# Attention and a feed-forward layer on one core: all weights converted during attention, x prepared in small pieces, each token tile visited once

## The chip, the core and the metric

The kernel runs on one core of one Trainium2 chip. The metric is the device time of one execution in microseconds, the median of 3 runs. The engines named below are those of the profile: PE (TensorE matmul, with its weight loads as PEld), DVE (VectorE), ACT (ScalarE), POOL (GpSimd) and SP (SyncE, whose queue issues every DMA here). Each engine runs its own instructions in order and waits for semaphores of the others.

## The reference

Causal attention with a decay over 8 batches x 8 heads x 576 positions x 64, then a feed-forward layer with a gate of its own on the 4608 tokens x 512:

```python
scores = (q @ k.T) / sqrt(64) + cum[:, None] - cum[None, :]     # cum = cumsum(log(clip(f, 1e-4, 1)))
attn = softmax(where(causal, -1e9, scores));  x = attn @ v       # -> 4608 tokens x 512
h = x @ w_in                                                     # 512 x 2048
out = (h * erf(softplus(h))) @ w_out                             # 2048 x 512
```

The weights arrive as 64-bit floats, and the kernel turns them into 32-bit floats itself with integer operations on the two words of each. Every feed-forward operand is split into a high part that TensorE multiplies as fp32r and a low part, and a product is three matmuls (high x high, high x low, low x high). The first product uses Strassen's scheme in Winograd's form: 7 products of halves instead of 8, so weights and x are combined (sums and differences of halves) before they are split.

## The kernel before, in words

**Attention** is a software pipeline over t = 0..68. One head pair has two values of t, 64 in all. In iteration t the kernel scales the probabilities of t-2 (normalize: two small DVE operations, L493 and L494, then 4 or 6 POOL operations, L498), copies out the result of t-5 (store), computes the scores of t (PE), reduces them on DVE while it adds the decay (L476), exponentiates those of t-1 (ACT), transposes those of t-3 (PE, copied out by ACT and DVE) and multiplies those of t-4 by v (PE). The result goes to xt_d in DRAM. At the end of an iteration stands one step of weight conversion: convert(u, step) for quarter u = 4a + i of the eight feature blocks a, four steps to a quarter. Half the weights (16 quarters, blocks 0 to 3) are converted here, from t = 4 on; they go to DRAM as wi_d[a] and wo_d[a].

**The feed-forward stage** is a list of 48 units, each one token tile (768 tokens) with one feature block (256 of 2048). In middle(u) PE does down(u), 36 matmuls of 512 columns into y; ACT does softplus and erf for unit u+1 (activate), DVE adds y into ys (flush, L250) and multiplies the gate (L210), ACT and POOL split the gate into gh and gl (round_gate, L217 and L218). Then PE does up(u+2), 42 matmuls of 384 columns. So PE alternates down and up, and gl(u+1) has to be there when down(u+1) begins.

The units are ordered in nine visits: tiles 0 to 2 with blocks 0 to 3, tiles 0 to 2 again with blocks 4 to 7, then tiles 3 to 5 with all eight. The partial sums of the first three visits go to DRAM (part_d) and are read back (want_y). In the first eleven units tasks() puts six conversion steps into each unit, for the other 16 quarters. x of the next visit is loaded with xt_d two units ahead (load_x), combined on POOL (combine_x, 768-element operations, L125) and split by split_x (ACT copies the high part, L144, POOL or DVE subtract it, L145), all of this around the last unit of a visit. For the first visit it is done in iterations 58 to 63 of attention.

The order on PE, DVE, ACT and POOL is the order in which the code is written; SP's order is left to a scheduler. Tile pools set who has to wait for a buffer: wop (the feed-forward layer's wo tiles), yp and ps_y are opened only when attention's pools are closed, on the same memory.

## Time and profile before

| | |
|---|---|
| median of 3 runs | 1215.16 us (1213.96 to 1215.73) |
| the profiled execution: time, span | 1214.0 us, 1212.2 us |
| mean granted TensorE clock | 0.965 |
| PE, DVE, ACT, POOL busy, share of the span | 91%, 68%, 58%, 54% |
| HBM read, written | 231.88 MB, 46.81 MB |
| down(0) begins; the last two downs run together (from the span's start) | 396.05 us; 16.38 us from 1192.12 |

How to read it: a row of a timeline has the start, the duration, the engine, the line, what is written and read, a count, and in brackets the engine's idle time ahead of it and who ended it. A row of a windows view has, for one stretch, its length, the busy time of PE, PEld, DVE, ACT and POOL with counts, the granted clock, the DMA engines' busy share and GB/s. The chain of waits follows the work that ended last back from the end: a row there is a start, a duration and what it was. A row of a group of instructions has its count, its summed time, the mean in ns of one, and the idle time ahead.

### The profile page before, as it was taken

What the parts mean: (1) busy time and instruction counts of PE and PEld (TensorE: products, weight loads), DVE (VectorE), ACT (ScalarE), POOL (GpSimd) and SP (SyncE); (2) the same over time, 40 slices, a digit from 0 to 9 for tenths busy, and PEclk for the clock granted to TensorE, in tenths of its full rate; (3) what the DMA queues carried; (4) which work ended last, traced back from release to release, by engine and by line L of the source; (5) the groups of instructions that cost most, each with busy time, mean ns of one, the idle gap of its engine ahead of it and who ended that gap; (6) DMA issues with size and microseconds to landing.
All of it is one profiled execution on the core that took longest, in us unless ns stands there. A gap on an engine that the chain in (4) does not pass through costs nothing.

```text
span 1212.2 us, 21632 instructions
## 1 busy us (share of the span) xinstructions
PE 1108.3 (91%) x7552; PEld 966.7 (80%) x7552; DVE 822.8 (68%) x1883; ACT 708.3 (58%) x1532; POOL 659.3 (54%) x691
## 2 busy tenths in 40 slices
PE   5999999999885968878779999999999999999998
PEld 3887878878674757767669888898999899989997
DVE  4788888888863667786856565656565666665565
ACT  3787777777774344545355655656556555665553
POOL 2566586585883575675673637283336533452233
PEclk7999999999998889888979999999999999999999
DMA  6689889798565458768669594948545855556532
GB/s 243 195 263 343 297 272 333 235 310 253 192 190 178 181 195 287 282 216 309 228 209 329 181 328 166 339 157 289 187 186 191 278 202 181 181 187 239 191 131 87
DMA packets 73420, 280.10 MB, mean 231 GB/s; under 512 B 7648, under 2 KB 16864, under 8 KB 61024
## 3 DMA queue, kind: packets, MB, share of 16 engines
q1 hardware_dynamic: 73312, 278.72, 66.3%
q8 instruction: 60, 0.98, 0.3%
q14 instruction: 48, 0.39, 0.1%
HBM read 231.88 MB, written 46.81 MB: 230 GB/s over the span
## 4 chain that ended last, share of the span: by engine, by line
PE 57%; POOL 18%; DVE 11%; issue 9%; DMA 3%; ACT 2%; SPq 0%; POOLq 0%; ACTq 0%; DVEq 0%
PE y L230 20%; PE s L453 7%; PE o L537 6%; PE pha L171 5%; PE phx L171 5%; PE phy L171 5%; PE t L510 5%; POOL gl L218 4%; POOL xs L145 4%; POOL rt L125 3%; DVE ys L250 2%; POOL pr L498 2%; PE phb L171 2%; POOL wa L381 2%; DVE e L210 2%
## 5 line engine op out<-in xcount | busy, mean ns | idle before, releaser
L218 POOL TENSOR_TENSOR gl<-e,gh 128x384 fp32r<-128x384 f32 x192 | 217.2, 1162 | 344.8 <-PE y L230 218.0
L230 PE MATMUL y<-wo,gh 128*128 128x512 f32 x1152 | 361.3, 395 | 30.1 <-DVE ys L250 17.2
L230 PEld LDWEIGHTS y<-wo,gh 128*128 128x128 f32 x1152 | 218.1, 191 | 76.4 <-DVE ys L250 20.2
L230 PE MATMUL y<-wo,gl 128*128 128x512 f32 x576 | 227.4, 395 | 0.0
L250 DVE TENSOR_TENSOR ys<-y,ys 128x512 f32<-128x512 f32 x252 | 172.9, 689 | 78.9 <-PE y L230 76.8
L498 POOL TENSOR_SCALAR pr<-pr,st 128x576 f32<-128x576 f32 (+4 forms) x320 | 166.6, 543 | 108.6 <-DVE st L494 96.9
L488 ACT ACTIVATE pr<-pr,st 128x576 f32<-128x576 f32 (+3 forms) x320 | 176.8, 557 | 8.4 <-DVE st L476 8.4
L476 DVE CUSTOM_DVE_ANT_0 pr<-s,c 128x576 f32<-128x576 f32 (+3 forms) x320 | 136.7, 487 | 51.9 <-PE s L458 44.8
L171 PE MATMUL pha<-xs,wi 128*128 128x384 f32 x576 | 123.6, 351 | 36.4 <-DVE u L181 35.5
L171 PEld LDWEIGHTS pha<-xs,wi 128*128 128x128 f32 x576 | 105.4, 195 | 45.6 <-DVE u L181 30.9
L217 ACT CAST gh<-e 128x384 fp32r<-128x384 f32 x192 | 92.3, 512 | 69.6 <-DVE e L210 69.2
L453 PE MATMUL s<-k,q 64*128 64x320 f32 (+4 forms) x768 | 117.3, 424 | 13.6 <-DMA k<-in_k_dram 8.3
L230 PEld LDWEIGHTS y<-wo,gl 128*128 128x128 f32 x576 | 109.6, 190 | 24.0 <-POOL gl L218 0.7
L171 PE MATMUL phx<-xs,wi 128*128 128x384 f32 x576 | 121.1, 346 | 0.3
L171 PE MATMUL phy<-xs,wi 128*128 128x384 f32 x576 | 118.7, 341 | 0.0
L510 PE MATMUL t<-ident,pr 128*128 128x128 f32 x800 | 106.8, 278 | 10.1 <-POOL pr L498 8.3
L519 ACT COPY pt<-t 128x512 f32<-128x512 f32 x128 | 73.6, 576 | 70.8 <-PE t L510 70.8
L200 ACT ACTIVATE e<-pha 128x384 f32<-128x384 f32 x48 | 23.5, 490 | 155.2 <-PE pha L171 155.2
L537 PE MATMUL o<-pt,v 128*64 128x128 f32 (+1 forms) x1920 | 104.6, 262 | 9.8 <-DVE xo L546 7.9
L177 DVE TENSOR_TENSOR u<-phx,u 128x384 f32<-128x384 f32 x96 | 53.6, 558 | 87.3 <-PE phx L171 85.1
L453 PEld LDWEIGHTS s<-k,q 64*128 64x128 f32 x768 | 77.0, 195 | 44.3 <-issue 28.3
L537 PEld LDWEIGHTS o<-pt,v 128*64 128x64 f32 x1920 | 95.8, 139 | 19.8 <-issue 6.5
(65 smaller groups left out, 1692.0 us busy)
## 6 DMA issues: line engine op xcount, KB each, us to landing
wi<-wi_d SPq DMA_DIRECT2D x48, 1792.0 KB, 7.4
wo<-wo_d SPq DMA_DIRECT2D x48, 1024.0 KB, 5.0
v<-in_vp_dram SPq DMA_DIRECT2D x32, 576.0 KB, 6.8
c<-cum_d SPq DMA_DIRECT2D x62, 288.0 KB, 5.5
r<-xt_d SPq DMA_DIRECT2D x36, 384.0 KB, 3.6
q<-in_q_dram SPq DMA_DIRECT2D x32, 320.0 KB, 4.4
k<-in_k_dram SPq DMA_DIRECT2D x32, 288.0 KB, 5.0
xt_d<-xo SPq DMA_DIRECT2D x32, 288.0 KB, 6.5
```

The lines of the kernel that those rows point to most:

```text
L171: nc.tensor.matmul(out=ps, lhsT=wi[:, w, n, kd], rhs=xs[:, x, kd], start=not part and kd == 0 and i == 0, stop=kd == 1 and i == 2, skip_gr ...
L217: nc.scalar.copy(out=gh, in_=e_)
L218: nc.gpsimd.tensor_tensor(out=gl, in0=e_, in1=gh.bitcast(F32), op=ALU.subtract)
L230: nc.tensor.matmul(out=y, lhsT=x[:, cs], rhs=wo[:, i, w], start=i == 0 and n == 0, stop=i == 1 and n == 2)
L250: nc.vector.tensor_tensor(out=ys, in0=y, in1=ys, op=ALU.add)
L453: nc.tensor.matmul(out=s[j][:, at:at + k1 - k0], lhsT=q[h, PAD + START[i]:PAD + END[i]], rhs=k[h, k0:k1], start=i > 0, stop=k1 < END[i])
L476: nc.vector.tensor_tensor_reduce(out=to[:, ::-1] if j else to, in0=score, in1=decay_, scale=-0.125, scalar=BIG, op0=ALU.add, op1=ALU.min, ...
L488: nc.scalar.activation(out=seg, in_=seg, func=AF.Exp, bias=st[:, 0, j, m:m + 1], scale=-1.0, accum_out=st[:, 1, j, m:m + 1])
L498: nc.gpsimd.tensor_scalar(out=seg, in0=seg, scalar1=st[:, 2, j, m:m + 1], scalar2=1.0, op0=ALU.mult, op1=ALU.mult)
L510: nc.tensor.transpose(out=b[:, n * P:(n + 1) * P], in_=probs[t][:, at:at + P], identity=ident)
L519: nc.scalar.copy(out=pt[:, 512 * a:512 * a + 512], in_=b)
L537: nc.tensor.matmul(out=o[h, to:to + width], lhsT=v[:, ch, h], rhs=pt[:, at[j]:at[j] + width], start=n == 0, stop=n == len(parts) - 1, skip ...
```

## The change

**Weights.** All 32 quarters are converted during attention, by a table of work with 70 slots: one slot at the end of each iteration from t = 4, two from t = 60 on. A quarter takes two slots: words (three DVE tensor_scalar operations) and joined (two DVE scalar_tensor_tensor operations), where before it took four steps with one POOL and four DVE operations. The combining and splitting of weights is cut into pieces over the following slots: combine (two 256-element POOL operations at a time), in_high and in_low (ACT, POOL: 512-element pieces in place of one of 1792 elements), out_high and out_low. The pool cv is closed with attention.

**x.** x_steps cuts the combining and splitting of one tile's x into 29 steps: 22 POOL operations of 384 elements and 7 ACT copies. For tile 0 they run one an iteration from t = 33; for the next tiles, prepare(u) puts up to five of them behind round_gate in the units a = 1 to 6 of the visit before. The pool xq gives odd tiles four more buffers. DVE takes no part in it any more.

**Visits.** There are six visits of eight units, so a tile's sums stay in ys, and part_d is gone.

```diff
...
-NU1 = 4
-HALF = 3
+X0 = 32
...
-TINY = float(np.array(0x38100000, np.uint32).view(np.float32))
+TINY = 2.0 ** -15
...
-        if part == 0:
...
+        def sub(name, a, b, kd):
+            if kd == 0 and name not in ("12",):
+                raw[v, name] = self.half(name, v)
+            nc.gpsimd.tensor_tensor(out=raw[v, name][:, kd], in0=raw[v, a][:, kd], in1=raw[v, b][:, kd], op=ALU.subtract)
+
+        def high(n, nm):
+            pool = self.xq if v % 2 and n > 2 else self.xp
+            self.xs[v, n] = x = pool.tile([P, 2, 2, TB], F32R, name=f"xs{v}_{n}", tag="xs",
+                                          bufs=10 if pool is self.xp else 4)
+            nc.scalar.copy(out=x[:, 0], in_=raw[v, nm])
+
+        def low(n, nm, kd):
+            x = self.xs[v, n]
+            nc.gpsimd.tensor_tensor(out=x[:, 1, kd], in0=raw[v, nm][:, kd], in1=x[:, 0, kd].bitcast(F32),
+                                    op=ALU.subtract)
+
+        steps = []
+        for name, a, b in (("T1", "12", "11"), ("T2", "22", "T1"), ("12", "22", "12")):
+            steps += [lambda args=(name, a, b, kd): sub(*args) for kd in range(2)]
+        for n, nm in enumerate(("11", "T2", "12", "T1", "21", "T4", "22")):
+            if n == 5:
+                steps += [lambda args=("T4", "21", "T2", kd): sub(*args) for kd in range(2)]
+            steps.append(lambda n=n, nm=nm: high(n, nm))
+            steps += [lambda args=(n, nm, kd): low(*args) for kd in range(2)]
+        return steps
...
-    def want_y(self, u):
...
-
     def flush(self, u, tb, y):
         nc = self.nc
-        k, a = self.units[u]
-        v, feats = self.visits[k]
-        ys = self.y[k][tb]
-        if a:
-            nc.vector.tensor_tensor(out=ys, in0=y, in1=ys, op=ALU.add)
+        v, a = divmod(u, NU)
+        if a == 0:
+            self.y[v, tb] = self.yp.tile([P, DM], F32, name=f"ys{v}_{tb}", tag="ys", bufs=8)
+            nc.vector.tensor_copy(out=self.y[v, tb], in_=y)
+            return
+        ys = self.y[v, tb]
+        nc.vector.tensor_tensor(out=ys, in0=y, in1=ys, op=ALU.add)
+        if a == NU - 1:
+            row = v * NW + tb * P
+            nc.sync.dma_start(out=self.out[row:row + P], in_=ys)
+
+    def prepare(self, u):
+
+        v, a = divmod(u, NU)
+        if v + 1 == NV:
+            return
+        if a == 0:
+            self.load_x(v + 1)
+            self.later = self.x_steps(v + 1)
         else:
-            nc.vector.tensor_copy(out=ys, in_=y)
-        if a == feats[-1]:
-            row = v * NW + tb * P
-            nc.sync.dma_start(out=self.out[row:row + P] if a == NU - 1 else self.part_d[v * NTB + tb], in_=ys)
-
-    def prepare(self, u):
...
-
-    def prepare_last(self, u):
...
-
-    def middle(self, u, tasks):
+            for _ in range(-(-len(self.later) // (NU - 1 - a)) if a < NU - 1 else 0):
+                self.later.pop(0)()
+
+    def middle(self, u):
...
         if more:
             for n in range(4):
                 self.round_gate(u + 1, n)
+            self.prepare(u)
...
-    cv = ctx.enter_context(tc.tile_pool(name="cv", bufs=2))
...
-    def convert(u, step):
...
+        cv = ph.enter_context(tc.tile_pool(name="cv", bufs=2))
...
+        def load_weight(u):
+
+            a, i = divmod(u, 4)
+            if a == NU:
+                return
+            r = (2 * a + i) * P
+            raw = cv.tile([P, 2 * DM], I32, name=f"wraw{u}", tag="wraw")
+            raws[u] = [raw.rearrange("p (n w) -> p n w", w=2)[:, :, w] for w in range(2)]
+            nc.sync.dma_start(out=raw, in_=w_in[a, i - 2] if i > 1 else w_out[r:r + P])
+
+        def words(u):
+
+            raw = raws[u]
+            tops[u] = top = cv.tile([P, DM], F32, name=f"wtop{u}", tag="wtop", bufs=3)
+            topi = top.bitcast(I32)
+            nc.vector.tensor_scalar(out=topi, in0=raw[1], scalar1=0x7FFFFFFF, scalar2=None, op0=ALU.bitwise_and)
+            nc.vector.tensor_scalar(out=top, in0=top, scalar1=TINY, scalar2=None, op0=ALU.max)
+            nc.vector.tensor_scalar(out=topi, in0=topi, scalar1=3, scalar2=0x3FFFFFFF,
+                                    op0=ALU.logical_shift_left, op1=ALU.bitwise_and)
+
+        def joined(u):
+
+            a, i = divmod(u, 4)
+            raw, topi = raws.pop(u), tops[u].bitcast(I32)
+            nc.vector.scalar_tensor_tensor(out=topi, in0=raw[0], scalar=29, in1=topi,
+                                           op0=ALU.logical_shift_right, op1=ALU.bitwise_or)
+            out_, top, sign = topi, topi, raw[1]
+            if i > 1:
+                if i == 2:
+                    sums[a] = cv.tile([P, 8, 2 * P], F32, name=f"wa{a}", tag="wa", bufs=1)
+                out_ = (sums[a][:, 4:6] if i == 3 else sums[a][:, ::7]).bitcast(I32)
+                top, sign = (x.rearrange("p (i n) -> p i n", i=2) for x in (top, sign))
+                del tops[u]
+            nc.vector.scalar_tensor_tensor(out=out_, in0=sign, scalar=-0x40000000, in1=top,
+                                           op0=ALU.bitwise_and, op1=ALU.bitwise_or)
+            load_weight(u + 2)
+
+        def out_high(a, i):
+            highs[a, i] = hi = cv.tile([P, DM], F32R, name=f"wohi{a}_{i}", tag="wohi", bufs=1)
+            nc.scalar.copy(out=hi, in_=tops[4 * a + i])
+            nc.sync.dma_start(out=wo_d[a][:, 2 * i * DM:(2 * i + 1) * DM], in_=hi.bitcast(F32))
+
+        def out_low(a, i):
+            top, hi = tops.pop(4 * a + i), highs.pop((a, i))
+            nc.gpsimd.tensor_tensor(out=top, in0=top, in1=hi.bitcast(F32), op=ALU.subtract)
+            nc.sync.dma_start(out=wo_d[a][:, (2 * i + 1) * DM:(2 * i + 2) * DM], in_=top)
+
+        def combine(a, *which):
+            w = sums[a]
+            for n in which:
+                x, y, op = {3: (7, 5, ALU.add), 2: (0, 7, ALU.subtract), 1: (3, 0, ALU.subtract),
+                            6: (4, 1, ALU.subtract)}[n]
+                nc.gpsimd.tensor_tensor(out=w[:, n], in0=w[:, x], in1=w[:, y], op=op)
+
+        def in_high(a, lo, hi):
+            highs[a] = part = cv.tile([P, 4, 2 * P], F32R, name=f"whi{a}_{lo}", tag="whi", bufs=1)[:, :hi - lo]
+            nc.scalar.copy(out=part, in_=sums[a][:, lo:hi])
+            nc.sync.dma_start(out=wi_d[a][:, lo * 256:hi * 256], in_=part.rearrange("p i f -> p (i f)").bitcast(F32))
+
+        def in_low(a, *which):
+            for lo, hi in which:
+                w = sums[a][:, lo:hi]
+                nc.gpsimd.tensor_tensor(out=w, in0=w, in1=highs[a][:, lo % 4:lo % 4 + hi - lo].bitcast(F32), op=ALU.subtract)
+                if hi == 7:
+                    nc.sync.dma_start(out=wi_d[a][:, 7 * 256:], in_=sums.pop(a)[:, :7].rearrange("p i f -> p (i f)"))
+
+        work = defaultdict(list)
+        for a in range(NU):
+            for i in range(4):
+                work[8 * a + 2 * i].append((words, 4 * a + i))
+                work[8 * a + 2 * i + 1].append((joined, 4 * a + i))
+            for i in range(2):
+                work[8 * a + 2 * i + 2].append((out_high, a, i))
+                work[8 * a + 2 * i + 3].append((out_low, a, i))
+            for n, args in enumerate([(combine, a, 3, 2), (combine, a, 1, 6), (in_high, a, 0, 4), (in_low, a, (0, 2), (2, 4)),
+                                      (in_high, a, 4, 7), (in_low, a, (4, 6), (6, 7))]):
+                work[8 * a + 8 + n].insert(0, args)
+        work = [work[n] for n in range(8 * NU + 6)]
...
+            if t == X0:
+                moe.load_x(0)
+                moe.later = moe.x_steps(0)
             if t == NH - 6:
-                moe.load_x(0)
                 moe.load_wi(0)
                 moe.load_wi(1)
-            if t == NH - 5:
...
-                    moe.prepare(1)
...
-            if t >= 4 and todo:
-                convert(*todo.pop(0))
+            for _ in range(1 if t < NH - 4 else 2):
+                if t >= 4 and work:
+                    for call, *args in work.pop(0):
+                        call(*args)
+            if t > X0 and moe.later:
+                moe.later.pop(0)()
...
     moe.wop = ctx.enter_context(tc.tile_pool(name="wop", bufs=1))
+    moe.xq = ctx.enter_context(tc.tile_pool(name="xq", bufs=1))
     moe.yp = ctx.enter_context(tc.tile_pool(name="yp", bufs=1))
...
-    def tasks():
...
-
     for u in range(moe.n):
-        moe.middle(u, tasks)
+        moe.middle(u)
         if u + 2 < moe.n:
-            moe.prepare(u + 2)
             moe.up(u + 2, 0)
             moe.up(u + 2, 1)
             moe.load_wi(u + 4)
-            moe.prepare_last(u + 2)
-    assert not todo
```

What this does to the order, at three places. In the rows, names end with the program's buffer numbers.

*The end of an attention iteration, DVE.* Before, the third step of a quarter stands ahead of L493 (pt is the copy out of the transposes, wraw and wtop a weight quarter, st the row sums):

```order
L517 COPY pt47_3971<-t47_2_3982 128x512
L515 COPY pt47_3971<-t47_3_3988 128x64
L375 TENSOR_SCALAR wraw11_3778<-wtop11_3859 128x512
L377 SCALAR_TENSOR_TENSOR wraw11_3778<-wraw11_3778 128x512
L493 TENSOR_SCALAR st49_3886<-st49_3886 128x6
L494 RECIPROCAL st49_3886<-st49_3886 128x6
```

Now words and joined stand there by turns, in every iteration:

```order
L333 TENSOR_SCALAR wtop20_3698<-wraw20_3450 128x512
L334 TENSOR_SCALAR wtop20_3698<-wtop20_3698 128x512
L335 TENSOR_SCALAR wtop20_3698<-wtop20_3698 128x512
L476 TENSOR_SCALAR st43_3565<-st43_3565 128x6
L477 RECIPROCAL st43_3565<-st43_3565 128x6
...
L342 SCALAR_TENSOR_TENSOR wtop20_3698<-wraw20_3450,wtop20_3698 128x512
L351 SCALAR_TENSOR_TENSOR wtop20_3698<-wraw20_3450,wtop20_3698 128x512
L476 TENSOR_SCALAR st44_3648<-st44_3648 128x4
L477 RECIPROCAL st44_3648<-st44_3648 128x4
```

On POOL the same iterations have, behind the scaling of the probabilities (L481), pieces of block 4's and 5's weights (wa, wtop) and of x (xs):

```order
L481 TENSOR_SCALAR pr45_3727<-pr45_3727,st45_3728 128x448 x2
L481 TENSOR_SCALAR pr45_3727<-pr45_3727,st45_3728 128x320 x2
L481 TENSOR_SCALAR pr45_3727<-pr45_3727,st45_3728 128x64 x2
L380 TENSOR_TENSOR wa4_3448<-wa4_3448,whi4_0_3862 128x512 x2
L362 TENSOR_TENSOR wtop20_3698<-wtop20_3698,wohi5_0_3869 128x512
L129 TENSOR_TENSOR xs0_2_3781<-r12_0_2613,xs0_2_3781 128x384
```

The small operation that frees the next scaling (L493 before, L476 now) stands behind the conversion on DVE, and behind it stand the next store and reduction.

*The last unit of a visit, POOL.* Before, five 768-element operations for the next visit's x (xs, rt) stand between the gl of one unit and those of the next:

```order
L218 TENSOR_TENSOR gl22_12_8913<-e22_12_8883,gh22_12_8912 128x384
L145 TENSOR_TENSOR xs6_0_8918<-r11_6_8613,xs6_0_8918 128x768
L145 TENSOR_TENSOR xs6_1_8921<-rt2_6_8775,xs6_1_8921 128x768
L145 TENSOR_TENSOR xs6_2_8924<-r12_6_8615,xs6_2_8924 128x768
L125 TENSOR_TENSOR rt4_6_8984<-r21_6_8619,rt2_6_8775 128x768
L145 TENSOR_TENSOR xs6_3_8986<-rt1_6_8773,xs6_3_8986 128x768
L145 TENSOR_TENSOR xs6_5_8992<-rt4_6_8984,xs6_5_8992 128x768
L218 TENSOR_TENSOR gl23_11_9064<-e23_11_9040,gh23_11_9063 128x384
```

Now a unit has at most five POOL pieces of 384 elements, here units 11 to 13:

```order
L212 TENSOR_TENSOR gl11_12_7221<-e11_12_7191,gh11_12_7220 128x384
L119 TENSOR_TENSOR r12_2_6931<-r22_2_6933,r12_2_6931 128x384
L129 TENSOR_TENSOR xs2_0_7225<-r11_2_6929,xs2_0_7225 128x384 x2
L212 TENSOR_TENSOR gl12_11_7356<-e12_11_7332,gh12_11_7355 128x384
L212 TENSOR_TENSOR gl12_21_7360<-e12_21_7336,gh12_21_7359 128x384
L212 TENSOR_TENSOR gl12_22_7364<-e12_22_7334,gh12_22_7363 128x384
L212 TENSOR_TENSOR gl12_12_7368<-e12_12_7338,gh12_12_7367 128x384
L129 TENSOR_TENSOR xs2_1_7229<-rT2_2_7080,xs2_1_7229 128x384 x2
L129 TENSOR_TENSOR xs2_2_7373<-r12_2_6931,xs2_2_7373 128x384 x2
```

The same work is spread over six units, and each piece stands behind a unit's own gl.

*The end of attention, SP.* The transfers take eight semaphores DMAHW0 to DMAHW7 in turn, each waiting for its own earlier use, so the last store to xt_d has DMAHW6 before:

```order
L151 DMA wi3_5372<-wi_d3_104 128x3584 [waits DMAHW3_49,PE_49]
L397 DMA wo_d3_112<-whi15_5394 128x512 [waits DMAHW4_49,Activation_49]
L398 DMA wo_d3_112<-wtop15_5163 128x512 [waits DMAHW5_49,Pool_49]
L552 DMA xt_d_82<-xo31_5374 128x576 [waits DMAHW6_49,DVE_49]
L346 DMA wraw17_5494<-in_w_in_dram 128x1024 [waits DMAHW7_49]
L157 DMA wo0_5416<-wo_d0_109 128x2048 [waits DMAHW2_49,DMAHW6_49,DMAHW0_49,PE_49]
```

Now it has DMAHW5, and the load of wo0 waits for others, among them (DMAHW3) the last write of weights:

```order
L375 DMA wi_d7_90<-whi7_4_5593 128x768 [waits DMAHW2_49,Activation_49]
L382 DMA wi_d7_90<-wa7_5229 128x1792 [waits DMAHW3_49,Pool_49]
L145 DMA wi3_5619<-wi_d3_86 128x3584 [waits DMAHW4_49,PE_49]
L535 DMA xt_d_82<-xo31_5621 128x576 [waits DMAHW5_49,DVE_49]
L151 DMA wo0_5659<-wo_d0_91 128x2048 [waits DMAHW3_49,DMAHW6_49,DMAHW2_49,DMAHW0_49]
```

The first wo load no longer waits for the last store to land, since wop lies where the weight conversion's buffers were.

More of the change, by code (lines that the diff above doesn't have):

```diff
@@ L93, in __init__ @@
         self.xt_d, self.out, self.xp, self.wp = xt_d, out, xp, wp
-        first, second, every = (list(range(*r)) for r in ((NU1,), (NU1, NU), (NU,)))
-        self.visits = ([(v, first) for v in range(HALF)] + [(v, second) for v in range(HALF)]
-                       + [(v, every) for v in range(HALF, NV)])
-        self.units = [(k, a) for k, (v, feats) in enumerate(self.visits) for a in feats]
-        self.n = len(self.units)
+        self.n = NV * NU
+        self.later = []
         self.raw, self.xs, self.wi, self.wo = {}, {}, {}, {}
@@ L222, in down @@
         nc = self.nc
-        k, a = self.units[u]
         wo, g = self.wo[u], self.g[u]
@@ L257, in prepare @@
-    def prepare(self, u):
-        k, a = self.units[u]
-        feats = self.visits[k][1]
-        left = len(feats) - 1 - feats.index(a)
-        if left == 2:
-            self.load_x(k + 1)
-        elif left == 1:
-            self.combine_x(k + 1, 0)
-        elif left == 0:
-            for n in range(3):
-                self.split_x(k + 1, n)
-    def prepare_last(self, u):
-        k, a = self.units[u]
-        if a == self.visits[k][1][-1]:
-            self.combine_x(k + 1, 1)
-            for n in range(3, 7):
-                self.split_x(k + 1, n, vector=n % 2 == 0)
@@ L322, in attention_moe @@
     xt_d = dram.tile([DM, NT], F32, name="xt_d")
-    part_d = [dram.tile([P, DM], F32, name=f"part_d{c}") for c in range(NTB * HALF)]
     wi_d = [dram.tile([P, 2 * 7 * 2 * P], F32, name=f"wi_d{a}") for a in range(NU)]
@@ L329, in attention_moe @@
     wp = ctx.enter_context(tc.tile_pool(name="wp", bufs=1))
-    cv = ctx.enter_context(tc.tile_pool(name="cv", bufs=2))
     moe = Moe(tc, xt_d, out, xp, wp)
-    moe.wi_d, moe.wo_d, moe.part_d = wi_d, wo_d, part_d
-    raws, sums = {}, {}
-    def load_weight(u):
-        a, i = divmod(u, 4)
-        if i < 2:
-            src = w_in[a, i]
-        else:
-            r = (2 * a + i - 2) * P
-            src = w_out[r:r + P]
-        raws[u] = raw = cv.tile([P, 1024], I32, name=f"wraw{u}", tag="wide")
-        nc.sync.dma_start(out=raw, in_=src)
@@ L402, in attention_moe @@
-    pieces = {1: [(u, i) for u in range(4 * NU1) for i in range(4)],
-              2: [(u, i) for u in range(4 * NU1, 4 * NU) for i in range(4)]}
+    moe.wi_d, moe.wo_d = wi_d, wo_d
     moe_pools = ctx.enter_context(ExitStack())
@@ L570, in attention_moe @@
         load(1)
-        todo = pieces[1]
         load_weight(0)
+        load_weight(1)
         for t in range(NH + 5):
@@ L632, in attention_moe @@
                 moe.ps_h = moe_pools.enter_context(tc.tile_pool(name="ps_h", bufs=1, space=PSUM, side="right"))
-        assert not todo and not pts and not held and not vals
+        assert not work and not moe.later and not pts and not held and not vals
     moe.wop = ctx.enter_context(tc.tile_pool(name="wop", bufs=1))
+    moe.xq = ctx.enter_context(tc.tile_pool(name="xq", bufs=1))
     moe.yp = ctx.enter_context(tc.tile_pool(name="yp", bufs=1))
@@ L639, in attention_moe @@
     moe.load_wo(1)
-    todo = pieces[2]
-    def tasks():
-        for _ in range(2):
-            if todo:
-                convert(*todo.pop(0))
     for u in range(moe.n):
-        moe.middle(u, tasks)
+        moe.middle(u)
         if u + 2 < moe.n:
-            moe.prepare(u + 2)
             moe.up(u + 2, 0)
```

105 lines of the change are left out of this document (7 added, 98 removed).

## The prediction, made before the changed kernel ran

> **What bounds the kernel now.** I read the page's head first, then the chain of waits in order of time, then busy times by stage.
>
> ```profile
> span 1212.2 us, 21632 instructions
> PE 1108.3 (91%) x7552; PEld 966.7 (80%) x7552; DVE 822.8 (68%) x1883; ACT 708.3 (58%) x1532; POOL 659.3 (54%) x691
> ```
>
> PE is the busiest engine by far, but 91% is a mean over stages that differ. The chain shows where PE waits:
>
> ```profile
> 374.37 8.39 issue
> ...
> 384.52 6.37 DMA xt_d<-xo
> 390.89 5.15 issue
> 396.05 10.56 PE y L230 x36
> ...
> 637.90 8.20 PE y L230 x36
> ...
> 1083.58 8.20 PE y L230 x36
> ...
> 1192.12 16.38 PE y L230 x72
> ```
>
> Each row "PE y x36" is the down of one unit; the last row holds the two last, so 1192.12 is unit 46 and 396.05 unit 0. From 1083.58 to 1192.12 are 7 units, 15.506 us each. The three long stages:
>
> ```profile
> 203.37:302.40 99.03, 97.29 (x1160) 81.28 (x1161) 84.51 (x315) 76.46 (x238) 65.39 (x111) 1.00 0.84 269
> 396.02:637.90 241.88, 195.45 (x859) 171.18 (x860) 176.04 (x245) 110.75 (x180) 157.88 (x113) 0.89 0.67 237
> 637.90:1192.12 554.22, 546.68 (x2732) 491.31 (x2731) 338.29 (x570) 313.21 (x526) 248.64 (x185) 1.00 0.61 217
> ```
>
> Attention (first row) keeps PE busy 98% of the time, with DVE at 85% and POOL at 66%. In the feed-forward stage up to 637.90, where weights are converted, PE is busy 81% at a clock of 0.89. After that PE is the bound, nearly without gaps.
>
> **The change part by part.**
>
> *Feed-forward stage.* 46 units lie between 396.05 and 1192.12: 796.07 us. At 15.506 they take 713.3. Counted back from the end, 637.90 is unit 11, so the eleven units with conversion take 241.85 in place of 170.6 (71.3 lost) and the other 35 lose 11.5, at the changes of visit. The change takes out both causes: no conversion, and no bunched x work in a visit's last unit. I keep the slow first down, 10.56 - 8.20 = 2.4, since PE still comes to it after a wait. Gain: 796.1 - 713.3 - 2.4 = **80.4 us**.
>
> What is added to a unit is x: at most five POOL pieces and two ACT copies. Their cover, in the timeline of a steady unit, and under it the two operations as groups over the whole span:
>
> ```profile
> 1089.77 4.66 POOL L218 TENSOR_TENSOR gl<-e,gh 128x384 fp32r<-128x384 f32 x4 [8.25 <-ACT gh L217]
> 1091.70 0.52 ACT L217 CAST gh<-e 128x384 fp32r<-128x384 f32 x1 [0.84 <-DVE e L210]
> 1097.10 0.49 ACT L200 ACTIVATE e<-pha 128x384 f32<-128x384 f32 x1 [4.88 <-PE pha L171]
> ...
> L145 POOL TENSOR_TENSOR xs<-r,xs 128x768 fp32r<-128x768 f32 x20 | 37.7, 1883 | 0.0
> L144 ACT CAST xs<-r 128x768 fp32r<-128x768 f32 x36 | 29.9, 831 | 0.0
> ```
>
> POOL's gl end at 1094.43 and the next unit's begin 15.5 after 1089.77, so 10.85 us are free; five pieces of half of 1883 ns are 4.7. ACT is free for 4.88 us; two copies of 0.83 are 1.7. One copy per visit, that of T4, waits for three POOL pieces, to about 1097.3, and ends at 1098.1, 1.0 after the next softplus could begin. But gl ends 10.85 us into the unit (1094.43 - 1083.58) and is needed at 15.5, so 4.6 us of slack take that. I cost x here at nothing. With that cover gone it would be 4.7 us in each of 30 units, 141 us.
>
> *The first wo load.* Before, it is issued at 390.89, when the last store has landed. Now it no longer waits for that store, so it can go out behind it, at 384.52; the last weights should be written by then, since their POOL pieces stand right behind the scaling of t = 63. Gain **6.4 us**, or 0 if those weights are late.
>
> *Attention.* The pace and what an operation costs there:
>
> ```profile
> 203.37 1.66 PE s L453 x12
> 213.21 1.66 PE s L453 x12
> ...
> 304.42 1.66 PE s L453 x12
> ...
> L377 DVE SCALAR_TENSOR_TENSOR wraw<-wraw 128x512 int32<-128x512 int32 x10 | 6.9, 695 | 0.3
> L366 DVE SCALAR_TENSOR_TENSOR wtop<-wtop,wraw 128x512 f32<-128x512 f32 x10 | 6.9, 695 | 0.0
> L362 POOL TENSOR_TENSOR wa<-wa 128x256 f32<-128x256 f32 x8 | 5.7, 732 | 0.2
> L395 POOL TENSOR_TENSOR wtop<-wtop,whi 128x512 f32<-128x512 f32 x5 | 6.4, 1283 | 11.6 <-DVE xo L550 11.6
> ...
> L375 DVE TENSOR_SCALAR wraw<-wtop x32: 412/422/4077, 47.7 to 628.7; 128x512 int32<-128x512 int32 x32
> ```
>
> The first three rows are the scores of t = 37, 39 and 57 in the chain; then come groups from 100 to 300 us, and last L375 over the whole span with its shortest, median and longest in ns. Undisturbed, an iteration takes (213.21 - 203.37)/2 = 4.92; over the 20 it is 5.05. DVE's conversion before, per quarter: one operation of 0.42 and three of 0.69, 2.5 us over four iterations, 0.62 each. Now: three tensor_scalar at 0.42 (L375's median; no row has the masking and the maximum, and I take them like it) and two of 0.69 over two iterations, 1.32 each. So DVE gets 0.70 more per iteration, and had (99.03 - 84.51)/20 = 0.73 idle. Alone that just fits, and nothing is left for waits.
>
> And there are waits. L375's last two figures, median and maximum, say that the same operation takes 0.42 or up to 4.08 us. The timeline shows with what:
>
> ```profile
> 86.31 3.99 POOL L381 TENSOR_TENSOR wa<-wa,whi 128x1792 f32<-128x1792 f32 x1
> 87.43 3.17 DVE L375 TENSOR_SCALAR wraw<-wtop 128x512 int32<-128x512 int32 x1
> ```
>
> DVE's operation ends 0.30 behind POOL's: it stood until POOL's was over. Behind it in DVE's queue stand L493, the next store and the next reduction, and for the reduction waits PE's next score. The pieces on POOL are shorter now, so one wait is at most 1.28, but there are more of them, and all five DVE operations of a quarter are of kinds that can meet them. Per block of eight slots POOL gets 4 x 0.73 (combine), 5 x 1.28 and 0.73 (in_low, out_low; L395 has the 512-element size): 10.1 us. Six such rounds lie in t = 12 to 59, 60.6; the first block's out_low adds 2.6 and some 20 pieces of x 18.8: 82 us of POOL work that the conversion on DVE can run into. Lower bound: DVE meets none of it, 0. Upper bound: all of it adds to DVE's full queue, 82. I take half, 41: POOL's pieces start when the scaling ends, just when DVE reaches its conversion, so they meet, but DVE's first operation can run ahead of some pieces, and pieces also run under the next store and reduction. The stalls of the 3.99 us operation go: (5.05 - 4.92) x 54 = 7. Cost **34 us** (bounds -7 and 75).
>
> *From t = 59 on.*
>
> ```profile
> 314.19 1.73 PE L453 MATMUL s<-k,q 64*128 64x448 f32 x12
> ...
> 343.83 1.73 PE L453 MATMUL s<-k,q 64*128 64x448 f32 x12
> ```
>
> These are t = 59 and 63: 29.6 us for four iterations where 19.7 is the pace, because x of tile 0 is prepared there. Now two slots an iteration stand in its place: 4 x 1.32 more on DVE and half of 10.1 of POOL, 19.7 + 5.3 + 5.0 = 30.0. No difference. Behind t = 63 the order on PE is the same, 0.
>
> *Sum*, against the profiled execution's 1214.0 (1.8 around its span): 1214.0 - 80.4 - 6.4 + 34 = 1161.2. The median of the runs stands 1.2 above that execution: **1162 us**.
>
> One rule of the Trainium skill bears on the half that I took. The page "SBUF — State Buffer", section "Who interferes with whom", says that GpSimd and VectorE share one pair of ports, held for a whole instruction by whichever starts first, and that VectorE needs it for a two-port tensor_scalar and, against a GpSimd operation that reads SBUF, for anything with two SBUF inputs. The rows of L381 and L375 agree for tensor_scalar. By this rule every operation of words and joined is exposed, which is the second rival below.
>
> **The rivals.**
>
> *Attention stays at PE's pace.* DVE's idle time is as large as what is added, and 512-element pieces block less than one of 1792. Against it: all of the idle time would have to be usable. Attention then costs -7: 1214.0 - 80.4 - 6.4 - 7 = 1120, with the median's 1.2, 1121.
>
> *Every piece on POOL is paid in full*, a lock step of DVE and POOL. For it: 87.43 waits out its POOL operation. Against it: means of 695 ns for L377 and L366 are far from 0.69 plus a POOL operation. Cost 75: 1202, with the median's 1.2, 1203.
>
> *Slower than before: the clock falls in attention.* PE would idle a part of each iteration, and where it idles its clock is lower:
>
> ```profile
> 374.00:396.00 22.00, 8.16 (x93) 7.41 (x91) 5.48 (x13) 7.64 (x13) 3.69 (x5) 0.79 0.64 223
> 430.00:460.00 30.00, 19.12 (x78) 16.55 (x78) 18.39 (x26) 15.84 (x27) 22.71 (x16) 0.83 0.64 224
> ```
>
> At PE 64% busy the clock is 0.83. The gains of 86.8 are eaten from 86.8/54 = 1.6 us per iteration on, a pace of about 6.6. If the lock step brings 4.92 + 82/54 = 6.4 and the clock falls to 0.7, PE's own 4.92 becomes 7.0: 54 x (7.0 - 5.05) = 105, 1214 - 86.8 + 105 = 1232, with the median's 1.2, 1233. Against it: at 6.4 PE would still be 77% busy, and at a clock of 0.83 its work takes 5.9, so PE isn't the bound.
>
> The Trainium skill's page "TensorE: Matmul & The Clock Gate", Part 1, gives a half clock after an idle window of about 3.4 us. By it, gaps of 1 to 2 us an iteration would hardly lower the clock and this rival would have almost no chance; the row of 430.00:460.00 is a mean and can't tell.
>
> **How the numbers follow.** Forecast (half is paid) 55%; attention at PE's pace 22%; paid in full 18%; clock 3%; 2% that something in the feed-forward stage takes back 50 us or more. The predicted time is the forecast's, 1162. The range goes from a tenth or so of POOL's pieces paid (1214 - 86.8 - 7 + 8 + 1.2 = 1130) to about nine tenths (1196). About 0.2%, 2.4 us, is what a measurement of this kernel can tell: faster 96%, within it 1%, slower 3%.
>
> **What would show it.** Downs 15.5 us apart from unit 1 to 46 without a step at a change of visit show the first term; the wo load issued right behind the last store shows the second. For attention: scores some 5.7 us apart between t = 12 and 59, tensor_scalar of words well above 0.42 in the mean, and PE about 87% busy. The forecast is wrong if scores stay 4.9 apart or go beyond 6.4, if gl ends later than 15 us into a unit, or if down(0) still waits for the store's landing.

## The result, and the profile after

The change made the kernel faster, by far less than forecast: 1200.64 us (1199.8 to 1201.78) against 1215.45 for the kernel before on the same chip, a ratio of 0.9881 (0.9864 to 0.9898). The forecast was 1162 with a range of 1130 to 1196. All times below are of executions in the faster of two states; one of e6's four, 1233.25 us at a clock of 0.848, was in the slower one and is left out (with it e6's median is 1158.64 in place of 1158.30).

The head of the profile of the changed kernel, then its chain of waits (start, duration, what):

```profile
span 1198.0 us, 21626 instructions
...
PE 1102.8 (92%) x7552; PEld 973.9 (81%) x7552; DVE 801.6 (67%) x1899; ACT 697.0 (58%) x1519; POOL 606.6 (51%) x732
```

```profile
454.25 7.49 DMA wo<-wo_d
461.98 10.79 PE y L223 x36
...
480.07 8.20 PE y L223 x36
...
1162.36 8.20 PE y L223 x36
...
1177.87 16.41 PE y L223 x72
```

The feed-forward stage is what the forecast said: from down(0) at 461.98 to unit 46 at 1177.87 are 715.9 us, where it was 796.1 before, so 80.2 were gained. But down(0) begins 65.9 us later than before (461.98 against 396.05), not 27.6. It lies in attention. The stretch from the scores of t = 12 to those of t = 59, after and before (length, busy PE, PEld, DVE, ACT, POOL, clock, share of the DMA engines, GB/s):

```profile
72.61:380.78 308.17, 254.83 (x2798) 215.19 (x2795) 255.49 (x823) 201.53 (x600) 210.14 (x316) 0.90 0.82 281
```

```profile
72.77:314.19 241.42, 234.12 (x2799) 195.22 (x2795) 204.51 (x752) 186.22 (x575) 162.79 (x268) 1.00 0.87 289
```

It took 66.8 us more. DVE got 51 us more of busy time in it, waits for POOL's pieces included, and yet is busy only 255 of 308 us: something makes DVE stand still. The waits of the changed kernel (who waits, for whom, total us, times, longest):

```profile
POOL pr L481 <- DVE st L477: 120.7, 40, 19.9
...
DVE wa L351 <- DMA wi_d<-wa: 40.3, 6, 7.5
PE o L520 <- DVE xo L533: 40.3, 13, 6.6
```

DVE waits for a DMA that *writes to* DRAM. Here is one of the six waits in the timeline, from the scores of t = 17 to those of t = 19:

```profile
101.22 2.01 PE L436 MATMUL s<-k,q 64*128 64x448 f32 x12
...
106.42 1.02 DVE L342 SCALAR_TENSOR_TENSOR wtop<-wraw,wtop 128x512 int32<-128x512 int32 x1
106.47 1.57 PE L436 MATMUL s<-k,q 64*128 64x320 f32 x12
...
108.95 0.42 SPq L382 DMA_DIRECT2D wi_d<-wa  x1
...
114.95 0.69 DVE L351 SCALAR_TENSOR_TENSOR wa<-wraw,wtop 128x512 int32<-128x512 int32 x1 [7.50 <-DMA wi_d<-wa]
...
115.56 0.16 DVE L476 TENSOR_SCALAR st<-st 128x4 f32<-128x4 f32 x1
...
115.75 0.18 DVE L477 RECIPROCAL st<-st 128x4 f32<-128x4 f32 x1
...
116.13 2.27 POOL L481 TENSOR_SCALAR pr<-pr,st 128x576 f32<-128x576 f32 x4 [6.87 <-DVE st L477]
116.16 0.21 DVE L533 COPY xo<-o 128x64 f32<-128x64 f32 x1
...
116.43 2.83 PE L520 MATMUL o<-pt,v 128*64 128x128 f32 x28 [6.49 <-DVE xo L533]
...
119.18 3.25 PE L436 MATMUL s<-k,q 64*128 64x448 f32 x12
```

The sums of a weight block (tile wa, 8 KB a partition) have a single buffer. joined for quarter i = 2 of block a stands in slot 8a + 5 and writes the first of them (L351). The last piece of block a - 1 stands in slot 8(a - 1) + 13, which is the same slot: in_low finishes there, and only then is the low half of the block written out (L382, issued at 108.95). The DMA still reads the buffer that L351 wants to write, so DVE waits until 114.95. Behind L351 in DVE's queue stand the reciprocal, for which POOL's scaling waits, and the store's copy, for which PE's values wait, and behind those the next scores: 12.71 us from score to score (106.47 to 119.18) in place of 4.9. This comes back every eight iterations, at t = 19, 27, 35, 43, 51 and 59, with intervals of 11.5 to 13.5 us, and a seventh time behind t = 63.

### The profile page after: what moved, and what is told of

The parts are those of the page before. It is cut to its first block, busy times and chain, and to the rows that moved or that the text cites. A ratio compares the mean times of both kernels' runs of the same rounds, so it can differ in the third digit from the quotient of the medians.

```text
span 1198.0 us, 21626 instructions
## 1 busy us (share of the span) xinstructions
PE 1102.8 (92%) x7552; PEld 973.9 (81%) x7552; DVE 801.6 (67%) x1899; ACT 697.0 (58%) x1519; POOL 606.6 (51%) x732
## 4 chain that ended last, share of the span: by engine, by line
PE 61%; DMA 1%; DVE 0%; issue 0%; SPq 0%
PE y L223 33%; PE pha L165 8%; PE phy L165 8%; PE phx L165 8%; PE phb L165 4%; DMA wo<-wo_d 1%; DVE ys L235 0%; SPq L535 0%; SPq L151 0%
## 5 line engine op out<-in xcount | busy, mean ns | idle before, releaser
L212 POOL TENSOR_TENSOR gl<-e,gh 128x384 fp32r<-128x384 f32 x192 | 221.9, 1188 | 415.9 <-PE y L223 215.0
L223 PE MATMUL y<-wo,gh 128*128 128x512 f32 x1152 | 357.5, 391 | 8.8 <-DMA wo<-wo_d 8.8
L481 POOL TENSOR_SCALAR pr<-pr,st 128x576 f32<-128x576 f32 (+4 forms) x320 | 164.4, 537 | 159.3 <-DVE st L477 120.7
L520 PE MATMUL o<-pt,v 128*64 128x128 f32 (+1 forms) x1920 | 116.8, 280 | 68.8 <-DVE xo L533 40.3
L520 PEld LDWEIGHTS o<-pt,v 128*64 128x64 f32 x1920 | 107.4, 151 | 79.7 <-DVE xo L533 62.4
L436 PE MATMUL s<-k,q 64*128 64x320 f32 (+4 forms) x768 | 128.7, 448 | 13.2 <-DMA k<-in_k_dram 8.5
L194 ACT ACTIVATE e<-pha 128x384 f32<-128x384 f32 x48 | 23.6, 491 | 178.5 <-PE pha L165 178.5
L436 PEld LDWEIGHTS s<-k,q 64*128 64x128 f32 x768 | 87.4, 208 | 45.5 <-issue 19.8
L165 PE MATMUL pha<-xs,wi 128*128 128x384 f32 x576 | 116.9, 337 | 0.6 <-DVE st L459 0.6
L165 PE MATMUL phy<-xs,wi 128*128 128x384 f32 x576 | 115.3, 334 | 0.0
L165 PE MATMUL phx<-xs,wi 128*128 128x384 f32 x576 | 115.3, 334 | 0.0
L194 ACT ACTIVATE e<-u 128x384 f32<-128x384 f32 x144 | 74.7, 522 | 56.0 <-DVE u L171 56.0
```

What stands on the lines that cost most here:

```text
L165: nc.tensor.matmul(out=ps, lhsT=wi[:, w, n, kd], rhs=xs[:, x, kd], start=not part and kd == 0 and i == 0, stop=kd == 1 and i == 2, skip_gr ...
L194: nc.scalar.activation(out=e_, in_=h[c], func=AF.Softplus)
L212: nc.gpsimd.tensor_tensor(out=gl, in0=e_, in1=gh.bitcast(F32), op=ALU.subtract)
L223: nc.tensor.matmul(out=y, lhsT=x[:, cs], rhs=wo[:, i, w], start=i == 0 and n == 0, stop=i == 1 and n == 2)
L436: nc.tensor.matmul(out=s[j][:, at:at + k1 - k0], lhsT=q[h, PAD + START[i]:PAD + END[i]], rhs=k[h, k0:k1], start=i > 0, stop=k1 < END[i])
L481: nc.gpsimd.tensor_scalar(out=seg, in0=seg, scalar1=st[:, 2, j, m:m + 1], scalar2=1.0, op0=ALU.mult, op1=ALU.mult)
```

## Experiments

**Theory W** (formed from this trace): the wait for the single buffer took what the forecast is short of; the rest of attention's loss is what the forecast called half of POOL's pieces. **Rival L** is the forecast's own second rival, the lock step in which every piece on POOL is paid; its 1203 is close to the measured time. **Rival K**: the intervals of 7 to 8.7 us two iterations ahead of each wait come from it as well.

### e1: a second buffer for the sums

```diff
-                    sums[a] = cv.tile([P, 8, 2 * P], F32, name=f"wa{a}", tag="wa", bufs=1)
+                    sums[a] = (cv if a % 2 else io).tile([P, 8, 2 * P], F32, name=f"wa{a}", tag="wa", bufs=1)
```

> The sums wa get a second buffer (blocks of even number from the pool that is closed after the last score), nothing else changes. Theory W (DVE stands in joined until the write of the block before, wi_d<-wa, has read the single buffer): the six score intervals of 11.5 to 13.5 us at t = 19, 27, ... 59 fall to 4.9 to 5.4 (-45.7 in all), and the 9.9 us from the last score to the first up to 5.0 (-4.9): 1200.6 - 50.6 = 1150, between 1145 and 1158. Theory L (lock step of DVE and POOL, every piece paid, the wait only stands where another would): no change worth the name, 1195 or more. Theory K (the intervals of 7 to 8.7 us two iterations earlier come from the same wait too, -18): 1132.

Measured: **1162.06** us (1161.76 to 1162.39), ratio 0.9557 (0.9537 to 0.9578). That is 38.6 less from the buffer alone: short of theory W's 50.6 and 4 us outside its range, but far from the others. L falls, since every piece on POOL is still there. K falls as well: its six intervals (t = 17, 25, ... 57) sum to 41.4 us, where it had some 29 in place of the changed kernel's 47.4. The stretch from t = 12 to 59, and the chain:

```profile
73.51:344.50 270.99, 245.02 (x2798) 208.11 (x2794) 262.49 (x817) 200.68 (x597) 210.09 (x313) 0.99 0.86 313
```

```profile
415.95 7.75 DMA wo<-wo_d
423.93 11.19 PE y L223 x36
442.42 8.20 PE y L223 x36
```

DVE has no wait for wi_d<-wa any more and is busy 262.5 of 271.0 us, 97%: it is the fullest engine of attention now (e8 tests what that costs). The stretch is 29.6 longer than before the change, and down(0) begins 27.9 later, where the forecast had 34 and 27.6. The granted clock is 0.99 in place of 0.90, so the low clock of the changed kernel came from PE's standstills. Less was gained than the waits and their neighbours summed to (50.6), because iterations that were undisturbed in the changed kernel are not any more: the intervals at t = 21, 23, 29 and 31, 4.9 us there, are 5.7 to 6.9 here. A wait that is taken out isn't all gain: what the other engines did during it has to be done later.

### e2 and e3: the wait made shorter and longer

e2 sends the write in two parts, the first two slots earlier; e3 makes it twice.

```diff
+                if hi in (4, 7):
+                    at = hi // 6 * 4
+                    nc.sync.dma_start(out=wi_d[a][:, (7 + at) * 256:(7 + hi) * 256],
+                                      in_=sums[a][:, at:hi].rearrange("p i f -> p (i f)"))
                 if hi == 7:
-                    nc.sync.dma_start(out=wi_d[a][:, 7 * 256:], in_=sums.pop(a)[:, :7].rearrange("p i f -> p (i f)"))
+                    del sums[a]
```

> One buffer as before, but the write wi_d<-wa goes out in two parts, four sevenths of it two slots earlier and three sevenths where the whole stood. Theory W: the wait is the landing of the last part, which is 3/7 of the size, so the 6.0 us from issue to landing become some 3, 7 waits fall by 2.5 to 3.4 us each: 1177 to 1184. Theory L: 1195 or more.

```diff
...
-                    nc.sync.dma_start(out=wi_d[a][:, 7 * 256:], in_=sums.pop(a)[:, :7].rearrange("p i f -> p (i f)"))
+                    for to in (wi_d[a][:, 7 * 256:], spare_d[a]):
+                        nc.sync.dma_start(out=to, in_=sums[a][:, :7].rearrange("p i f -> p (i f)"))
+                    del sums[a]
```

> One buffer, and the write wi_d<-wa is made twice (the second into a spare array that nothing reads), so the buffer is held about twice as long. Theory W: each of 7 waits grows by 5 to 6 us: 1235 to 1243. Theory L: the wait is not what sets the pace, 1200 to 1210.

Measured: e2 **1188.03** (1184.49 to 1191.59), ratio 0.9771 (0.9741 to 0.9801); e3 **1216.50** (1214.27 to 1218.36), ratio 1.0013 (1.0000 to 1.0026). Both moved the way W says, by less than was expected. The waits of DVE at this operation, of e2 and of e3:

```profile
DVE wa L351 <- DMA wi_d<-wa: 22.9, 5, 6.2
DVE wa L351 <- ACT pr L475: 3.4, 1, 3.4
DVE wa L351 <- ACT pt L506: 1.5, 1, 1.5
```

```profile
DVE wa L352 <- DMA spare_d<-wa: 60.2, 7, 11.1
```

Two of e2's seven waits are put down to ACT. I count them with the others, because DVE starts 0.22 us behind the landing of the write in both (111.56 behind 111.34, 400.78 behind 400.56). So it is with a wait of 2.6 us at t = 63 in the changed kernel (415.97 behind 415.85). So the waits at this line sum to 0 in e1, 27.8 in e2, 42.9 in the changed kernel (40.3 + 2.6) and 60.2 in e3, and the times are 1162.1, 1188.0, 1200.6 and 1216.5. Counted from e1, each us of wait costs 0.93, 0.90 and 0.90 us; with the times of the profiled executions, from which the waits are, 0.80, 0.88 and 0.93. What I had wrong is how much the edit moves the wait: the two writes of e3 are issued 0.4 us apart and run side by side, the second lands only 2.1 to 3.0 us behind the first, and a wait is 2.5 us longer, not 5 to 6. With the shorter last write of e2 (three sevenths) a wait is only 2.2 us shorter.

### e4: the low halves left out

On e1's kernel, without the POOL subtractions of in_low and out_low:

```diff
-            nc.gpsimd.tensor_tensor(out=top, in0=top, in1=hi.bitcast(F32), op=ALU.subtract)
...
-                nc.gpsimd.tensor_tensor(out=w, in0=w, in1=highs[a][:, lo % 4:lo % 4 + hi - lo].bitcast(F32), op=ALU.subtract)
```

> As e1, and the six POOL subtractions of a block that make the low halves (in_low, out_low) are left out, so the low halves that are written are not the reference's; DVE's work, the copies on ACT and all DMAs stay. Theory W: what is left of the attention's excess in e1 is DVE waiting out these pieces, above all in the intervals of 7 to 8.7 us at t = 17, 25, ... 57 where two in_low and an out_low stand: some 18 to 25 us less than e1, about 1130. If the pieces cost nothing: the same as e1 within 3. Theory L: 40 us or more less than e1, since 7.2 of the 10.1 us of POOL pieces a block are gone.

Measured: **1127.14** us (1124.52 to 1130.74), 34.9 less than e1. Of the 37.7 between the profiled spans, 22.1 lie between t = 12 and 59 and 9.9 between the scores of t = 63 and the down of unit 1. Between W and L by its total; by the stretch it is W. The 9.9 are another thing: with its weights ready sooner, e4 issues the first wo load at 381.48, ahead of the last store (386.47), and PE doesn't wait for wo any more. The stretch of e4; then over the same stretches three groups of DVE operations in e1, and the three that answer to them in e4 (count, busy, mean ns):

```profile
71.87:320.81 248.94, 238.16 (x2799) 201.56 (x2795) 236.35 (x819) 199.24 (x596) 159.00 (x276) 1.00 0.94 339
```

```profile
L342 DVE SCALAR_TENSOR_TENSOR wtop<-wraw,wtop 128x512 int32<-128x512 int32 x24 | 31.2, 1300 | 0.0
L476 DVE TENSOR_SCALAR st<-st 128x4 f32<-128x4 f32 (+1 forms) x47 | 21.0, 446 | 0.0
...
L351 DVE SCALAR_TENSOR_TENSOR wtop<-wraw,wtop 128x512 int32<-128x512 int32 x12 | 16.5, 1374 | 0.4
```

```profile
L342 DVE SCALAR_TENSOR_TENSOR wtop<-wraw,wtop 128x512 int32<-128x512 int32 x24 | 25.9, 1081 | 0.0
...
L351 DVE SCALAR_TENSOR_TENSOR wtop<-wraw,wtop 128x512 int32<-128x512 int32 x12 | 10.8, 897 | 0.4
...
L473 DVE TENSOR_SCALAR st<-st 128x4 f32<-128x4 f32 (+1 forms) x47 | 9.2, 196 | 1.9 <-ACT pr L468 1.9
```

DVE's own instructions are the same, and 26.1 us of its busy time are gone (262.5 to 236.4): operations that stood until a piece on POOL was over. The largest part, 11.8 us, is L476, the small operation on st that opens the next iteration and stands right behind the conversion: in e1 all 13 instances of it above 0.4 us in this stretch end 24 to 30 ns behind the end of a piece on POOL.

### e5: the wo loads ahead of the fourth wi load

```diff
-                if t == NH + 3:
-                    moe.load_wi(3)
...
     moe.load_wo(1)
+    moe.load_wi(3)
```

> As e1, and the load of the fourth wi (1.8 MB, issued 3.8 us ahead of the first wo load and still running then) is issued behind the first two wo loads. Theory W2 (the first wo load lands 7.75 us after its issue instead of 4.8 because it shares the transfer engines with that load): down(0) 2.9 us earlier, 1159. Rival (the last store and the last write of weights hold it up, or up(3) comes late): 1162 as e1, or more.

Measured: **1164.06** (1162.87 to 1164.63). It says nothing on the question: SP's order is the scheduler's, and the fourth wi load stayed where it was, as SP's row of issues shows (L145 ahead of the last store, L535, and of the wo loads, L151):

```profile
414.27 0.32 SPq L145 DMA_DIRECT2D wi<-wi_d  x1
417.59 0.32 SPq L535 DMA_DIRECT2D xt_d<-xo  x1
418.09 19.03 SPq L151 DMA_DIRECT2D wo<-wo_d  x3
```

With every engine's order as in e1, the 2.0 us between them are what one and the same order differs by from one measurement, on another chip, to the next.

### e6: the pieces spread evenly

```diff
-                work[8 * a + 2 * i + 3].append((out_low, a, i))
-            for n, args in enumerate([(combine, a, 3, 2), (combine, a, 1, 6), (in_high, a, 0, 4), (in_low, a, (0, 2), (2, 4)),
-                                      (in_high, a, 4, 7), (in_low, a, (4, 6), (6, 7))]):
+                work[8 * a + 2 * i + 4].insert(0, (out_low, a, i))
+            for n, args in enumerate([(combine, a, 3, 2), (combine, a, 1, 6), (in_low, a, (0, 2)), (in_low, a, (2, 4)),
+                                      (in_low, a, (4, 6)), (in_low, a, (6, 7))]):
...
+            work[8 * a + 10].insert(0, (in_high, a, 0, 4))
+            work[8 * a + 12].insert(0, (in_high, a, 4, 7))
```

> As e1, with the same POOL pieces laid out evenly: in_low one piece to a slot (slots 2, 3, 4, 5 of a block of eight), out_low in slots 4 and 6, instead of three pieces in slot 3 and three in slot 5. Theory A (a DVE operation waits out one piece at most, so three pieces in one slot cost more than one each in three): 5 to 10 us less than e1, 1152 to 1157, and the longest of L342 and L351 near 1.3 us still. Theory B (DVE is full, each piece meets some DVE operation wherever it stands): 1160 to 1164. Theory C (pieces in the slots of words meet tensor_scalar operations that were free till now): 1165 to 1175.

Measured: **1158.30** us (1157.07 to 1158.98), ratio 0.9531 (0.9514 to 0.9548): 3.8 less than e1, and 5.8 less than e5, which has e1's order and was measured on the same chip as e6. That lies between A and B. But A's sign didn't come: the longest L342 is 1.78 us, as in e1 (1.80). And what C feared did happen: the second operation of words meets the pieces (e1, then e6):

```profile
L334 DVE TENSOR_SCALAR wtop<-wtop 128x512 f32<-128x512 f32 x23 | 12.3, 534 | 0.8
```

```profile
L334 DVE TENSOR_SCALAR wtop<-wtop 128x512 f32<-128x512 f32 x23 | 24.6, 1069 | 0.8
```

Against these 12.3 us stand 11.9 that the small operation on st gives back (mean 446 ns in e1, 195 here): the waits have mostly moved from one operation to another.

### e7: x of the next tile in one unit

```diff
-            for _ in range(-(-len(self.later) // (NU - 1 - a)) if a < NU - 1 else 0):
+            while self.later and a == NU - 3:
                 self.later.pop(0)()
```

> As e1, but all 23 steps of x of the next tile stand in one unit, the fifth of its visit's eight... units before its last two (a = NU - 3), instead of three to five in each unit. By the forecast's working (POOL's gl of the next unit then ends 20 pieces of 1.04 us later, with 10.85 + 4.65 us of room): 25.5 us of POOL in a unit of 15.5, 10 late, 4.6 of it slack, so 5.4 us at each of 5 changes of visit: 1189. If x is hidden even so: 1162. If POOL's delay runs on into the unit after it: 1200 or more.

(The steps are 29, 22 of them on POOL, not 23 and 20.) Measured: **1225.75** (1222.17 to 1226.36), ratio 1.0090 (1.0073 to 1.0106), 63.7 more than e1. The chain around one change of visit:

```profile
503.28 7.54 PE y L223 x33
...
512.16 2.00 POOL gl L212 x2
514.15 3.89 POOL rT L119 x4
...
521.89 7.76 POOL xs L129 x8
529.65 1.91 POOL rT L119 x2
533.14 1.62 ACT e L194 x4
534.79 1.28 ACT L196
537.32 2.29 PE pha L165 x6
...
546.21 8.20 PE y L223 x36
```

Two units lie between these downs, 31.0 at PE's pace; they took 42.9, so 11.9 are lost, and five times that is 60. The chain doesn't run over a late gl, as I had reckoned, but over ACT: its copy of T4 stands in ACT's queue until POOL has made T4 at 531.6, and the next unit's softplus (L194) stands behind that copy. So x costs nothing in the change only because its steps are spread: the cover was real, and thinner at ACT than I priced it.

### e8: a copy moved from DVE to ACT

```diff
-            elif a == 2:
-                nc.vector.tensor_copy(out=pt[:, 1024:1536], in_=b)
```

> As e1, but the third copy of an iteration from PSUM (pt, 0.69 us on DVE) is made by ACT (0.57 us), which is 74% busy between t = 12 and 59 while DVE is 97% busy. Theory D (DVE's own full queue, with the waits in it, sets attention's pace): 48 x 0.69 = 33 us come off DVE there, of which the floor of PE (238 of 271) leaves 20 to 30: 1132 to 1142. Theory E (the pace is set by the chain from score to score, in which a wait on POOL stands, and not by DVE's sum): 1158 to 1165. If ACT's exponentials come late through the added copy: over 1165.

Measured: **1150.63** (1148.54 to 1152.73), ratio 0.9470 (0.9451 to 0.9488), 11.4 less than e1 and between D and E. The stretch of t = 12 to 59, and a wait of PE over the whole span:

```profile
72.31:336.47 264.16, 240.10 (x2798) 201.40 (x2794) 228.63 (x779) 222.30 (x648) 214.92 (x311) 0.98 0.89 321
```

```profile
PE o L518 <- DMA v<-in_vp_dram: 20.4, 10, 2.9
```

DVE gave up 33.9 us of work and the stretch only 6.8 (4.1 more came from t = 59 to 63). DVE is at 87%, and loads of v that come late take its place: within the stretch PE's waits for the store's last copy (xo, L533 in e1) fall from 20.7 to 1.4 us, and those for v rise from 2.8 to 18.3. Why v comes late was not taken apart.

### e9, e10, e11: conversion done sooner, and all together

e9 is e1 with two slots an iteration from t = 56; e10 adds e8, e11 adds e8 and e6.

```diff
-            for _ in range(1 if t < NH - 4 else 2):
+            for _ in range(1 if t < NH - 8 else 2):
```

> As e1, but two slots of conversion an iteration from t = 56 on instead of 60, so that the last write of weights goes out some four slots earlier and both first wo loads stand in SP's queue ahead of the last two stores and of the fourth wi load. Theory W3 (the first wo load is late because it stands behind the last write of weights, which comes late, and shares the transfer engines with the fourth wi load): down(0) no longer waits for wo; it follows the last values and the store's copy, some 8 us earlier, and the four iterations t = 56 to 59 pay what t = 65 and 66 no longer do: 1152 to 1156. Rival (the last store's landing or PSUM holds down(0) there anyhow): 1160 to 1164.

> e8 and e9 in one (third copy of an iteration on ACT, conversion done four iterations sooner). If the two gains are apart from each other: 1162 - 11.4 - 8 = 1143, between 1139 and 1147. If ACT, 84% busy in e8, is what the earlier slots run into: 1148 or more.

> e6, e8 and e9 in one. With the 3.4 us of e6: 1139 (1135 to 1145). If with DVE relieved it no longer matters where the pieces on POOL stand: as e10 within 2.

Measured: e9 **1158.61** (1156.51 to 1159.87), ratio 0.9531 (0.9507 to 0.9555), e10 **1151.80** (1147.96 to 1154.80), e11 **1138.23** (1134.66 to 1140.53), ratio 0.9363 (0.9333 to 0.9392): the best of all, 62 us under the changed kernel. e9's 3.5 less than e1 is neither W3's 1152 to 1156 nor the rival's 1160 to 1164, and little beside the 2.0 of e5. But W3's step is there: in e9 the wait for wo is gone. Its chain, and the wait that is left:

```profile
422.51 5.81 DMA xt_d<-xo
429.19 3.02 PE y L223 x12
439.51 8.20 PE y L223 x36
```

```profile
DVE ys L232 <- DMA xt_d<-xo: 6.0, 1, 6.0
```

Down(0) has six parts of six matmuls, one for each 128 tokens. Four of them now run under the last store; only DVE's first copy into ys waits for that store to land, since ys lies on memory that attention used. From the scores of t = 63 to the down of unit 1 it is 55.9 us in place of e1's 69.3, a gain of 13.4; but t = 12 to 59 takes 6.8 us more and t = 59 to 63 4.2 more. Of the 6.8, 3.5 lie behind t = 55 and are, with the 4.2, the work that was moved. The other 3.3 lie ahead of t = 55, where every engine and SP's queue have e1's order, so they are not the edit's. e10 against e8 shows the same: 14.2 gained behind t = 63, 4.1 (most of it ahead of t = 55) and 8.0 lost ahead of it, and so no better: 1151.8 where 1143 was expected. The branch "1148 or more" has the number; that ACT is the cause is not shown. In e11 t = 12 to 59 takes 258.6 us, against 268.2 in e10: spreading the pieces is worth 9.0 by the spans and 13.6 by the medians once DVE has room, and 3.8 (5.8 against e5) while DVE is full. Why it is worth more then was not taken apart. That e11 came out at the 1139 expected is luck in part: of the terms of that sum the step from e8 to e10 gave nothing, and the spreading gave more.

## Why the prediction was right and wrong

**Feed-forward stage, -80.4: right.** Measured -80.2, units 15.51 us apart with no step at a change of visit. The claim that x is covered there holds: gl ends 11.0 us into every unit from 1 on, where 10.85 was reckoned and 15.5 is the limit. It is borne out by the other side too: put into one unit, x costs 12 us at each of five changes (e7). Of the two queues that could break the cover, ACT's breaks first: its copy of T4, reckoned 1.0 us late and covered, waits 9.25 us for POOL there.

**Attention, +34: the step that failed.** Measured +66.8 from t = 12 to 59. The step "Lower bound: DVE meets none of it, 0. Upper bound: all of it" took POOL's pieces for all that DVE could come to wait for. The new table of work also brings the last reader of a block's single buffer, a DMA of 0.9 MB, into the same slot as the next block's first writer, and I did not compare the two slots. With a second buffer the stretch is +29.6 and the whole kernel 1162.06, so the terms that I did reckon add up to what was forecast. The agreement to 0.1 us is luck: +29.6 came for +34, and the wo term missed the other way.

**Half of POOL's pieces: right in size.** In e1 the pieces that e4 leaves out take 31.7 + 20.6 = 52.3 us on POOL in this stretch (rows below), and leaving them out frees 26.1 us of DVE and 22.1 of the stretch. The pieces are stretched themselves here (L362 takes 1715 ns in the mean, 1276 in e6): at the forecast's 1.28 and 0.73 us they are 42.8, and the share is 61%. That is for these pieces alone; combine and x were not left out in any run.

```profile
L380 POOL TENSOR_TENSOR wa<-wa,whi 128x512 f32<-128x512 f32 (+1 forms) x24 | 31.7, 1344 | 0.0
...
L362 POOL TENSOR_TENSOR wtop<-wtop,wohi 128x512 f32<-128x512 f32 x12 | 20.6, 1715 | 0.0
```

The page "SBUF — State Buffer" of the Trainium skill, section "Who interferes with whom", has it that a DVE instruction with two SBUF inputs contends with a POOL instruction that reads SBUF. The groups under e4 agree with it for L342 and L351: 1300 and 1374 ns with these pieces, 1081 and 897 without. That every operation is exposed doesn't mean that every piece is paid.

**The first wo load, -6.4: wrong, 0 in the changed kernel and about -1.4 in e1.** It is issued right behind the last store, as forecast (454.25, behind a store at 453.75), but then takes 7.5 us in place of 5.15, and the store itself is issued 44.05 us behind the scores of t = 63 instead of 40.7. The seventh wait falls there, but it is about half of that: in e1, without it, the store is still 42.3 behind. So 3.9 us were lost at the issue and 2.3 in the transfer. The alternative "or 0 if those weights are late" has the number but not the cause: the last write of weights (issued at 449.20) lands at 453.12, ahead of the store's issue. The fourth wi load (issued 450.43, landed 458.57) and the last store (landed 459.29) run beside it. That these two stretch the load is argued, not shown: e5 did not move the wi load. e4 and e9 show that all of the wait for wo goes once the weights end sooner and the load is issued ahead of the last store.

**From t = 59 on, 0: right.** 28.9 us for four iterations, where 30.0 were forecast and 29.6 it was.

**The rivals.** The lock step gave 1203 and the time came out at 1200.6, for another reason: the near hit of a number is no evidence for its mechanism. The clock did fall, to 0.90 over the stretch, but behind the standstills: without them it is 0.99 (e1), and PE, busy 254.8 of 308.2 us, was not the bound. Of the signs that I named, one did its work: scores beyond 6.4 us apart (308.17/47 = 6.6) said that attention was mispriced, and the waits said where. Another was off: the tensor_scalar of words were to be well above 0.42 in the mean, and are 0.51 to 0.53; it is the scalar_tensor_tensor of joined that wait, with means of 1.30 and 1.38 on wtop where 0.69 was reckoned.

## What to carry to other kernels

When a table of slots or a pipeline is re-laid, list for every single-buffered tile the slot of its last reader and the slot of its next writer, and count the landing of a DMA that reads it: a write to DRAM that nobody waits for holds its source all the same, and an in-order engine that wants the buffer stops with all that is queued behind it. Price the queue behind the waiting instruction, not only the engine that is shared: both here and with x in one unit, an operation that itself took under 1 us held up the next unit's or iteration's first operation. And where a full engine bounds a stage, relieving it uncovers the next bound (late loads of v), and edits that were worth little alone can be worth more together.
